# One bank pair and contiguous copies for the last remainder of a spectral stage, with a new order of the stages around it

## The chip, the cores and the metric

The kernel runs on one core of a Trainium2 chip. The metric is the device time of one execution in microseconds. Five engines work side by side, each through its own list of instructions in order: PE (matrix products; "PEld" is its weight load), DVE and ACT (element-wise work, and the copies out of PSUM), POOL (element-wise work in SBUF) and SP, which here only issues DMAs. PSUM has eight banks; the kernel uses them as four pairs, named 0, 2, 4 and 6 by their first bank.

## The reference

One block with two halves: a filter in the frequency domain, and a gated feed-forward network, each with a residual.

```python
def _A_ref(x, w_r, w_i):
    X = rfft2(x.astype(float32))
    X = X * (w_r + 1j * w_i)
    return irfft2(X, s=(S, D)).astype(bfloat16)

def _B_ref(x, w_gate, w_up, w_down):
    return (gelu(x @ w_gate) * (x @ w_up)) @ w_down

h  = x + _A_ref(layernorm(x), w_r, w_i)
h2 = h + _B_ref(layernorm(h), w_gate, w_up, w_down)
```

S is 2048 rows, D 576 columns, the hidden width 4608; everything is bf16.

## The kernel before

The two-dimensional transform and its inverse are done as matrix products with cosine and sine tables, in stages; the feed-forward half follows.

**First stage** (order SEQ1): the rows are normalized and multiplied by ATAB into U. It ends near 20 us.

**Forward stage** (order SEQF, 16 tiles i = 0 to 15, GORD[i] is the frequency group). A capital letter issues the first part of a step's products, the small letter the second part and the copy out of PSUM. D and d (10 products of 288 columns) turn U into CUS. B (4 products) turns CUS into YS. T (two DVE instructions, L673) multiplies YS by the filter weights WS: the first 256 columns go to TP, the last 32 of the 288 to TR, where four tiles i stand side by side. V and v (two times 8 products of 128 columns, L681) turn TP into the main part of the inverse's input, V. R and r (L697) do the same for the remainder, TR, four tiles at once. The lists DENG, BENG, VENG and RENG say which engine copies (`ev`, L606): a V copy is either one instruction of 512 columns or two of 256, one each on ACT and DVE.

**The remainder.** Group 0 (tile 15, LAST) needs other tables than the others, so the last remainder is done in two steps: R3 for tiles 12 to 14, and R4 for tile 15 alone, on bank pairs of their own. Remainders 0 to 2 are copied to RB in one piece (128x256) and spread to VR by eight small DMAs each, three issued by SP and five by POOL. R3 and R4 are copied straight to VR: each tile takes two instructions of 32 partitions x 128 elements, ACT for tiles 12 and 15, DVE for 13 and 14. VR holds, per group, `[o][e][n]` with n (16 long) innermost; the source runs over n with e (4 long) innermost.

**Bank pairs.** A step of the forward stage that opens (D, B, V, R) takes the free pair that was named longest ago in SEQF; the small letter gives it back. The inverse stage does the same over SEQ (`SLOT`), and starts from the list `last`, which says in which order the pairs become free.

**Inverse stage** (order SEQ, row blocks c = 0 to 7): I (4 products, main part only, L829) and i (6 products, of which the last two read the remainder VR) give PS, which E copies to GS (engine by its suffix: A for ACT, D for DVE, S for half each). N and o (4 products each, L846) give the rows back; a adds them to XO on DVE (L852). s sums the squares (A: ACT, L855; D: DVE, L912), q and c make the reciprocal deviation (ACT, DVE), n normalizes into HN (L880; P: POOL, D: DVE), u and U transpose by products (L898), e copies to HT. G0 and G1 are the first gate and up products (L938) on the first four row blocks.

**Loads.** LOADS ties DMAs on SP to steps: with "hold", SP waits until the last product issued so far is done. In the inverse stage these are the ten parts of the feed-forward weights of slot 0 (parts 2 to 7 with I0, i1, N0, i3, o1, N3; parts 8 and 9 with o3) and the tables DP and ITD (with i7). The first product of G0 needs all ten parts. Row blocks 8 to 15 of the inverse are done later, between the gate and up products.

After G1 the feed-forward half runs four blocks of 512 rows: gate and up products (L938), their gelu and multiply, and the down products (L1038).

Of the kernel before, what the change touches and what calls it, by code (L numbers as in the profile page):

```python
# [4 lines left out]
BF16 = mybir.dt.bfloat16  # L5
# [19 lines left out]
LORD = "x0-2 x2-4 a0-4 x4-8 a4-8 x8-12 x12-16 a8-16".split()  # L25
SPLIT = tuple(int(w[1:-1]) for w in SEQ1 if w[0] == "F")
ACT_TILES = tuple(int(w[1:]) for w in SEQ1 if w[0] == "Q")
SEQF = """D0 D2 d0 D1 d2 d1 D3 B0 d3 B2 D5 B1 d5 D6 T0 B3 d6 T1 D4 V0 T2 d4 D8 v0 B5 d8 T3 D7 T5 B4 d7 V2 V1 v2 v1 D9 B6 T4 d9 D11 B8 d11 D10 B7 T6 d10 V3 V4 v3 R0 v4 r0 V6 T7 B9 v6 D12 B10 d12 T8 T9 R1 D13 r1 d13 V5 B11 v5 T11 D15 B12 d15 V7 V8 v7 D14 T10 v8 d14 B13 T12 R2 V10 r2 v10 B15 T13 B14 T15 V11 V9 v11 V12 v9 v12 T14 V15 V13 v15 V14 v13 v14 R3 R4 r3 r4""".split()
VENG = [('act', 'dve'), ('dve',), ('act',), ('act', 'dve'), ('act', 'dve'), ('act', 'dve'), ('act', 'dve'), ('act',), ('act', 'dve'), ('act',), ('act', 'dve'), ('act',), ('act',), ('act', 'dve'), ('act', 'dve'), ('act', 'dve')]
DENG, BENG = ['act', 'dve', 'act', 'dve', 'act', 'act', 'act', 'act', 'act', 'act', 'act', 'dve', 'act', 'act', 'act', 'act'], ['act', 'act', 'act', 'act', 'act', 'dve', 'act', 'act', 'act', 'act', 'dve', 'act', 'act', 'act', 'act', 'act']  # L30
LOADS = {"r0": "t", "v12": "0", "v15": "1", ".I0": "2", ".i1": "3", ".N0": "4", ".i3": "5", ".o1": "6", ".N3": "7", ".o3": "8 9", ".i7": "d"}
RENG = ['act', 'act', 'dve', 'act', 'act']
QR = ((0, 1), (1, 2), (2, 3), (3, 4), (4, 8), (8, 16))
DEF0, DSTEP = 3, 4
SEQ = """I0 I1 I2 i0 i1 E0S i2 N0 E1D I3 o0 i3 E2A N1 a0 N2 E3S o1 s0A o2 I5 a1 N3 i5 o3 a2 a3 q0 s1A I7 I6 c0 i6 s2D E5A q1 E6A i7 I4 N5 i4 o5 E7A N6 c1 n0P u0 q2 s3D E4A n1P o6 q3 U0 a5 c2 u1 e0A N4 U1 e1A c3 n3P n2D o4 u2 U2 N7 a6 u3 o7 a4 a7 U3 e2A G0 e3D G1""".split()


def _np_bf16(a):
# [8 lines left out]
def build_tables():  # L47
# [7 lines left out]
    T = {}  # L55
# [44 lines left out]
    for st in range(2):  # L100
        g = 1 - st
        for p in range(128):
            half, r, jj = p // 64, (p % 64) // 4, p % 4
            low = (g + 16 * jj) if half == 0 else _minus_rows(g)[jj]
            k = 128 * r + low
            w = np.exp(-2j * np.pi * ((k * nn) % 2048) / 2048.0)
            if low in (0, 64):
# [3 lines left out]
                c = np.conj(w)  # L111
# [220 lines left out]
def _build(nc, A_x, A_w_r, A_w_i, B_w_gate, B_w_up, B_w_down, out):  # L332
    P = Prog(nc)
    T = build_tables()
    dram = {n: nc.inline_tensor(_np_bf16(T[n]), name="c_" + n.lower()) for n in T}
    PE, DVE, ACT, SP, POOL = "pe", "dve", "act", "sp", "pool"
# [3 lines left out]
    sb = SbufMap(nc, base, top)  # L340
# [12 lines left out]
    VR = sb.alloc("VR", [128, NG, 2, 4, NT], BF16)  # L353
# [57 lines left out]
    TR = sb.alloc("TR", [128, 2, 2, 2, 128], BF16)  # L411
# [66 lines left out]
    GORD = list(range(1, NG)) + [0]  # L478
# [102 lines left out]
    for w in SEQ1:  # L581
        a = w[1:]
# [6 lines left out]
    LAST = NG - 1  # L589

    FB, used, busy = {}, {0: -8, 2: -7, 4: -6, 6: -5}, set()
    for t, w in enumerate(SEQF):
        k, i = w[0], w[1:].rstrip("abc")
        if k in "DBVR":
            b = min((b for b in used if b not in busy), key=lambda b: used[b])
# [4 lines left out]
        elif k in "dvr":  # L600
            b = FB[k.upper(), int(i)]
# [3 lines left out]
    def ev(eng, dst, src, r, w):  # L605
        fn = (lambda v: v.tensor_copy(dst, src)) if eng == DVE else (lambda a: a.activation(dst, src, ACTF.Copy))  # L606
        P.op(eng, fn, r=r, w=w)
# [68 lines left out]
    def st_V(i, second, engs):  # L676
        g, z, b0 = GORD[i], i % NZ, FB["V", i]

        def mm(h, o, ct, first, last, after):
            c, t_ = ct  # L680
            return P.op(PE, lambda t: t.matmul(bank(b0 + o, 0, 128, 128 * c, 128 * c + 128), TP[64 * h:64 * h + 64, z, o, t_, c:256:2], VT[64 * h:64 * h + 64, 0 if g else 1 + o, t_, :],  # L681
                                               start=first, stop=last), r=[("T", z), "VT"], w=[("PS", b0 + o)], after=after)

# [6 lines left out]
            ev(e, v5[:, n * a:n * a + n], banks(b0 + a, n, 256).rearrange("p a (c e) -> p a c e", e=4), [("PS", b0 + a + k) for k in range(n)], [("V", g, a + k) for k in range(n)])  # L690

    def st_R(q, second):
        js = [i for i in range(4 * q, 4 * q + 4) if i < LAST] if q < 4 else [LAST]
        g0, n, b0 = GORD[js[0]], len(js), FB["R", q]

        def mm(h, o, t_, first, last, after):
            return P.op(PE, lambda t: t.matmul(bank(b0 + o, 0, 128, 0, 128), TR[64 * h:64 * h + 64, min(q, 3) % 2, o, t_, :], VT[64 * h:64 * h + 64, 3 if q < 3 else 1 + o if q == 4 else 0, t_, :], start=first, stop=last),  # L697
                        r=[("TR", min(q, 3) % 2, j) for j in range(4)] + ["VT"], w=[("PS", b0 + o)], after=after)

        halves(("R", q), second, [[0, 1]] * 2, mm)  # L700
# [99 lines left out]
    vkeys = vmain + vtail  # L800


    SLOT, last, held, ing = {}, [-4, -3, -2, -1], set(), False
    for t, w in enumerate(SEQ):
        k, i = w[0], int(w[1:].rstrip("ADSP"))
        if k in "INu":
            b = min((b for b in range(2 * ing, 4) if b not in held), key=lambda b: last[b])
# [3 lines left out]
        elif k in "ioUEae":  # L811
            b = SLOT[{"i": "I", "o": "N", "U": "u", "E": "I", "a": "N", "e": "u"}[k], i] // 2
# [4 lines left out]
        elif k == "G":  # L817
            ing = True
# [131 lines left out]
    def gu_first(i):  # L950
        for a in range(4):
# [104 lines left out]
    for tb in range(4):  # L1056
# [26 lines left out]
        for w in "0 1 0 2 1 3 2 3".split() if tb < 3 else "0 1 0 2 1 2".split():  # L1083
            first = ("Z", tb, int(w)) not in ends
# [39 lines left out]
```

## Time and profile before

| | us |
|---|---|
| median of 3 runs (488.22 to 489.38) | 489.23 |
| profiled execution, device time | 489.5 |
| its span | 487.7 |
| PE busy | 477.5 (98%) |
| DVE busy | 185.0 (38%) |
| ACT busy | 147.9 (30%) |
| POOL busy | 53.0 (11%) |

Busy shares are means over the whole span; the first 60 us, where the change lies, look quite different from the feed-forward half. A PE that is busy is not at its peak: products are pipelined, and their ends are modelled. In rows by stretch, each engine's busy time stands with its count of instructions, and after them the granted clock of PE as a share of full speed, the DMA share and the GB/s. In rows by group, after the bar, stand the total busy time, the mean of one in ns, and the idle time before them with what ended it.

### The profile page before, as it was taken

The page shows a single profiled execution, that of the slowest core. Times are in us where ns is not written, and L with a number is a line of the kernel's source. Part 1 is how long each engine was busy: PE and PEld are TensorE (multiplying, and loading weights), DVE is VectorE, ACT ScalarE, POOL GpSimd, SP SyncE. Part 2 cuts the span into 40 slices and gives each one's busy share as a digit, 9 for nine tenths or more (in the row PEclk, how much of TensorE's full clock was granted, in tenths as well). Part 3 has the DMA queues.
Part 4 walks back from the last instruction along what each step waited for, and adds up shares of the span by engine and source line. Part 5 has one row for each costly group of instructions (what it writes and reads, how often), then busy time and mean ns, then how long its engine had stood idle before and what let it go on. Part 6 is the DMA issues. An engine that isn't in the chain of part 4 may idle for free.

```text
span 487.7 us, 12880 instructions
## 1 busy us (share of the span) xinstructions
PE 477.5 (98%) x5871; PEld 279.1 (57%) x5872; DVE 185.0 (38%) x367; ACT 147.9 (30%) x294; POOL 53.0 (11%) x87
## 2 busy tenths in 40 slices
PE   7997999999999999999999999999999999999998
PEld 3876765554477744444577644444677444444774
DVE  7897845656511134333300144333101233333011
ACT  6997754343400023233200022332100123323000
POOL 6873226010120000000000000000000000000000
PEclk9998999999999999999999999999999999999999
DMA  8954688971250001100000001000000000000000
GB/s 291 215 138 147 202 280 247 389 158 26 98 175 25 15 24 23 23 0 1 1 15 13 27 21 23 13 1 2 1 15 26 14 1 0 1 1 1 3 26 26
DMA packets 26966, 33.06 MB, mean 68 GB/s; under 512 B 12560, under 2 KB 19104, under 8 KB 26912
## 3 DMA queue, kind: packets, MB, share of 16 engines
q1 hardware_dynamic: 23248, 19.74, 14.7%
q0 software_dynamic: 3664, 12.50, 7.9%
q8 instruction: 46, 0.75, 0.7%
q14 instruction: 8, 0.07, 0.0%
HBM read 26.08 MB, written 2.36 MB: 58 GB/s over the span
## 4 chain that ended last, share of the span: by engine, by line
PE 94%; DMA 1%; DVE 1%; POOL 1%; SPq 0%; issue 0%; POOLq 0%; DVEq 0%
PE PS L938 57%; PE PS L1038 27%; PE PS L640 2%; PE PS L1050 2%; PE PS L681 2%; DMA XO<-in_A_x_dram 1%; PE PS L551 1%; PE PS L660 1%; PE PS L829 1%; PE PS L988 1%; DVE XO L852 1%; DVE VR L606 1%; POOL HN L880 1%; SPq L242 0%; PE PS L1005 0%; PE PS L846 0%
## 5 line engine op out<-in xcount | busy, mean ns | idle before, releaser
L938 PE MATMUL PS<-HT,WG 64*128 64x512 bf16 (+1 forms) x2142 | 233.3, 372 | 0.0
L946 ACT ACTIVATE GL<-PS 128x512 bf16<-128x512 f32 x144 | 85.7, 596 | 281.6 <-PE PS L938 281.6
L938 PEld LDWEIGHTS PS<-HT,WG 64*128 64x128 bf16 x2142 | 105.0, 94 | 115.1 <-DVE AT L947 0.2
L947 DVE TENSOR_TENSOR AT<-GL,PS 128x512 bf16<-128x512 bf16 x144 | 98.9, 687 | 165.7 <-ACT GL L946 165.7
L1038 PE MATMUL PS<-WD,AT 64*128 64x288 bf16 x2160 | 132.9, 283 | 0.0
L1038 PEld LDWEIGHTS PS<-WD,AT 64*128 64x128 bf16 x2160 | 102.5, 94 | 30.6
L1025 DVE TENSOR_TENSOR OS<-PS,XO 128x288 bf16<-128x288 f32 (+2 forms) x32 | 13.2, 453 | 125.5 <-PE PS L1038 118.0
L938 PE MATMUL PS<-HT,WGX 64*128 64x512 bf16 x486 | 53.4, 376 | 0.0
L938 PEld LDWEIGHTS PS<-HT,WGX 64*128 64x128 bf16 x486 | 23.0, 94 | 29.4
L855 ACT ACTIVATE OS<-XO,NM 128x576 bf16<-128x576 bf16 x14 | 10.8, 774 | 11.4 <-DVE XO L1009 11.4
L640 PE MATMUL PS<-FT,U 64*128 64x288 bf16 x160 | 13.2, 283 | 0.0
L551 PE MATMUL PS<-ATS,XO 128*128 128x128 bf16 x96 | 8.2, 219 | 2.9 <-POOL ATS L520 1.9
L673 DVE TENSOR_TENSOR TP<-YS,WS 128x1024 bf16<-128x1024 bf16 x16 | 11.0, 687 | 0.0
L562 ACT ACTIVATE U<-PS 128x384 bf16<-128x384 f32 (+2 forms) x31 | 10.5, 421 | 1.2 <-PE PS L551 0.9
L494 DVE BATCH_NORM_STATS2 ST<-XO 128x6 f32<-128x288 bf16 x26 | 9.9, 442 | 1.9 <-DMA XO<-in_A_x_dram 1.9
L829 PE MATMUL PS<-DT,V 64*128 64x288 bf16 x64 | 7.2, 333 | 3.0 <-DVE VR L606 2.9
L681 PE MATMUL PS<-VT,TP 64*128 64x128 bf16 x256 | 9.7, 217 | 0.0
L242 POOL DMA_DIRECT2D WG<-in_B_w_gate_dram x9 | 6.1, 679 | 33.1 <-DMA WG<-in_B_w_gate_dram 29.6
L242 POOL DMA_DIRECT2D WD<-in_B_w_down_dram x9 | 6.7, 757 | 25.4 <-PE PS L1005 25.4
L551 PEld LDWEIGHTS PS<-ATS,XO 128*128 128x128 bf16 x96 | 6.9, 98 | 4.3 <-POOL ATS L520 2.8
L606 ACT ACTIVATE YS<-PS 128x576 bf16<-128x576 f32 x14 | 9.0, 657 | 0.3 <-PE PS L660 0.2
L1050 PE MATMUL PS<-WD,AT 128*128 128x448 bf16 (+1 forms) x72 | 9.0, 286 | 0.0
(89 smaller groups left out, 237.8 us busy)
## 6 DMA issues: line engine op xcount, KB each, us to landing
WD<-in_B_w_down_dram POOLq DMA_DIRECT2D x9, 576.0 KB, 11.4
WG<-in_B_w_up_dram SPq DMA_DIRECT2D x6, 576.0 KB, 6.9
WG<-in_B_w_gate_dram POOLq DMA_DIRECT2D x6, 576.0 KB, 5.8
out_dram<-OS SPq DMA_DIRECT2D x30, 72.0 KB, 1.7
XO<-in_A_x_dram SPq DMA_DIRECT2D x3, 576.0 KB, 7.3
WG<-in_B_w_gate_dram SPq DMA_DIRECT2D x4, 288.0 KB, 3.5
WG<-in_B_w_up_dram SPq DMA_DIRECT2D x4, 288.0 KB, 3.4
WGX<-in_B_w_up_dram SPq DMA_DIRECT2D x2, 576.0 KB, 4.7
```

The lines of the kernel that those rows point to most:

```text
L242: fn = lambda e: e.dma_start(out_ap, in_ap)
L551: P.op(PE, lambda t, b=b, lhs=lhs, p0=p0, p1=p1, s=s, e=e, o=o, c=c: t.matmul(bank(b, p0, p1, o, o + 128), lhs, ATS[:, c, :], start=s, sto ...
L606: fn = (lambda v: v.tensor_copy(dst, src)) if eng == DVE else (lambda a: a.activation(dst, src, ACTF.Copy))
L640: return P.op(PE, lambda t: t.matmul(bank(b0 + o, 0, 128, 0, 2 * HK), U[64 * h:64 * h + 64, us, 2 * i:2 * i + 2, :, :], FT[64 * h:64 * h + ...
L681: return P.op(PE, lambda t: t.matmul(bank(b0 + o, 0, 128, 128 * c, 128 * c + 128), TP[64 * h:64 * h + 64, z, o, t_, c:256:2], VT[64 * h:64 ...
L829: e[o] = P.op(PE, lambda t, r0=r0, o=o, j=j, lhs=lhs: t.matmul(bank(b + o, 0, 128, 0, KW), lhs, DT[r0:r0 + 64, 2 * o + j if j < 2 else 4, ...
L938: op = P.op(PE, lambda t, h0=h0, kt=kt, wt=wt, b=b, s=(not second and j == 0), e=(second and j == n - 1): t.matmul(bank(b, 0, 128, c0, c1) ...
L946: P.op(ACT, lambda a: a.activation(GL[:, s2, :], bank(b0), ACTF.Gelu_apprx_tanh), r=[("PS", b0)], w=[("GL", s2)])
L947: P.op(DVE, lambda v: v.tensor_tensor(AT[:, f, :], GL[:, s2, :], bank(b0 + 1), op=ALU.mult), r=[("GL", s2), ("PS", b0 + 1)], w=[("AT", f)])
L1025: P.op(DVE, lambda v: v.tensor_tensor(OS[:, p % 2, d0:d1], bank(b, 0, 128, 0, d1 - d0), XO[:, c, d0:d1], op=ALU.add), r=[("PS", b), ("X", ...
L1038: e[h] = P.op(PE, lambda t, f=f, h=h, r0=r0, j=j: t.matmul(bank(b0 + h, 0, 128, 0, 288), AT[r0:r0 + 64, f, 128 * p:128 * p + 128], WD[r0:r ...
L1050: P.op(PE, lambda t, b=b, d0=d0, d1=d1, f=f, j=j: t.matmul(bank(b, 0, 128, 0, d1 - d0), AT[:, f, 128 * p:128 * p + 128], WD[:, f, d0:d1], ...
```

## The change

1. R3 now holds all four tiles, 12 to 15, and R4 is gone. Its products run twice over TR: part 0 with the table of the other groups into columns 0 to 127 of the bank pair, part 1 with the tables of group 0 into columns 128 to 255; tile 15 is copied from part 1. The number of products is the same.
2. VTAB gets six blocks instead of four, since all remainder tables are now kept in the order `[e][n]`. With that, the copies to VR read 64 contiguous columns and write 64 contiguous elements.
3. `last`, the order in which the inverse stage takes the pairs, is computed from the forward stage.
4. SEQF, its engine lists and SEQ are new orders of the same steps. In SEQ, one more E is split over both engines, all four n go to POOL, one s moves from DVE to ACT, and i7 (with DP and ITD) now stands ahead of o3 (with parts 8 and 9).

```diff
-SEQF = """D0 D2 d0 D1 d2 d1 D3 B0 d3 B2 D5 B1 d5 D6 T0 B3 d6 T1 D4 V0 T2 d4 D8 v0 B5 d8 T3 D7 T5 B4 d7 V2 V1 v2 v1 D9 B6 T4 d9 D11 B8 d11 D10 B7 T6 d10 V3 V4 v3 R0 v4 r0 V6 T7 B9 v6 D12 B10 d12 T8 T9 R1 D13 r1 d13 V5 B11 v5 T11 D15 B12 d15 V7 V8 v7 D14 T10 v8 d14 B13 T12 R2 V10 r2 v10 B15 T13 B14 T15 V11 V9 v11 V12 v9 v12 T14 V15 V13 v15 V14 v13 v14 R3 R4 r3 r4""".split()
+SEQF = """D2 D0 d2 D1 d0 d1 B2 D5 B0 d5 T2 D3 B1 d3 D4 T0 T1 B5 d4 D8 B3 d8 D7 T3 B4 d7 V0 D6 v0 V1 T5 d6 v1 R0 V2 r0 v2 T4 B6 D9 B8 T6 V3 d9 D11 v3 d11 B7 D10 B9 d10 V6 V4 T7 v6 v4 V5 B10 v5 R1 D12 T8 r1 d12 B11 T9 V7 D14 v7 T10 d14 D13 B12 d13 D15 T11 V9 T12 d15 v9 V8 B13 v8 R2 r2 T13 B14 T14 B15 V12 V10 v12 v10 V13 V11 T15 v13 V14 v11 v14 V15 R3 v15 r3""".split()
...
-RENG = ['act', 'act', 'dve', 'act', 'act']
+RENG = ['dve', 'act', 'act', 'act', 'act']
...
-SEQ = """I0 I1 I2 i0 i1 E0S i2 N0 E1D I3 o0 i3 E2A N1 a0 N2 E3S o1 s0A o2 I5 a1 N3 i5 o3 a2 a3 q0 s1A I7 I6 c0 i6 s2D E5A q1 E6A i7 I4 N5 i4 o5 E7A N6 c1 n0P u0 q2 s3D E4A n1P o6 q3 U0 a5 c2 u1 e0A N4 U1 e1A c3 n3P n2D o4 u2 U2 N7 a6 u3 o7 a4 a7 U3 e2A G0 e3D G1""".split()
+SEQ = """I0 I1 I2 i0 E0S i1 E1S i2 E2A N0 I3 o0 i3 N1 I4 o1 a0 E3S N2 o2 a1 s0A q0 i4 a2 s1A I7 c0 N3 E4S q1 s2D i7 I6 o3 E7A i6 c1 N4 o4 a3 q2 E6A c2 N7 I5 o7 a4 n0P N6 s3A a7 i5 n1P n2P q3 c3 o6 u1 U1 u2 E5A u0 U2 a6 n3P e1A e2D U0 N5 u3 e0A o5 a5 U3 G0 e3D G1""".split()
...
     def st_R(q, second):
-        js = [i for i in range(4 * q, 4 * q + 4) if i < LAST] if q < 4 else [LAST]
-        g0, n, b0 = GORD[js[0]], len(js), FB["R", q]
...
-            return P.op(PE, lambda t: t.matmul(bank(b0 + o, 0, 128, 0, 128), TR[64 * h:64 * h + 64, min(q, 3) % 2, o, t_, :], VT[64 * h:64 * h + 64, 3 if q < 3 else 1 + o if q == 4 else 0, t_, :], start=first, stop=last),
...
+        js = range(4 * q, 4 * q + 4)
+        b0 = FB["R", q]
...
+            part, t_ = pt
+            return P.op(PE, lambda t: t.matmul(bank(b0 + o, 0, 128, 128 * part, 128 * part + 128), TR[64 * h:64 * h + 64, q % 2, o, t_, :], VT[64 * h:64 * h + 64, 4 + o if part else 3, t_, :], start=first, stop=last),
...
-                dst = VR[64 * t_ + 32 * (j % 2):64 * t_ + 32 * (j % 2) + 32, g, :, :, :].rearrange("p o e n -> p o n e")
-                src = PS[32 * j:32 * j + 32, b0 * 512:(b0 + 2) * 512].rearrange("p (a c) -> p a c", a=2)[:, :, 64 * t_:64 * t_ + 64].rearrange("p a (n e) -> p a n e", e=4)
+                dst = VR[64 * t_ + 32 * (j % 2):64 * t_ + 32 * (j % 2) + 32, g, :, :, :].rearrange("p o e n -> p o (e n)")
+                src = PS[32 * j:32 * j + 32, b0 * 512:(b0 + 2) * 512].rearrange("p (a c) -> p a c", a=2)[:, :, 128 * (i == LAST) + 64 * t_:128 * (i == LAST) + 64 * t_ + 64]
                 ev((ACT, DVE, DVE, ACT)[j], dst, src, keys, [("V", g, 2 + t_)])
...
-    SLOT, last, held, ing = {}, [-4, -3, -2, -1], set(), False
+    SLOT, last, held, ing = {}, [sorted(used.values()).index(used[2 * b]) - 4 for b in range(4)], set(), False
```

DENG, BENG and VENG also change: of the 32 copies of D and B, DVE makes four instead of five; of the V copies, it makes three whole ones instead of one, and ACT four instead of five.

More of the change, by code (lines that the diff above doesn't have):

```diff
@@ L27 @@
 ACT_TILES = tuple(int(w[1:]) for w in SEQ1 if w[0] == "Q")
-SEQF = """D0 D2 d0 D1 d2 d1 D3 B0 d3 B2 D5 B1 d5 D6 T0 B3 d6 T1 D4 V0 T2 d4 D8 v0 B5 d8 T3 D7 T5 B4 d7 V2 V1 v2 v1 D9 B6 T4 d9 D11 B8 d11 D10 B7 T6 d10 V3 V4 v3 R0 v4 r0 V6 T7 B9 v6 D12 B10 d12 T8 T9 R1 D13 r1 d13 V5 B11 v5 T11 D15 B12 d15 V7 V8 v7 D14 T10 v8 d14 B13 T12 R2 V10 r2 v10 B15 T13 B14 T15 V11 V9 v11 V12 v9 v12 T14 V15 V13 v15 V14 v13 v14 R3 R4 r3 r4""".split()
-VENG = [('act', 'dve'), ('dve',), ('act',), ('act', 'dve'), ('act', 'dve'), ('act', 'dve'), ('act', 'dve'), ('act',), ('act', 'dve'), ('act',), ('act', 'dve'), ('act',), ('act',), ('act', 'dve'), ('act', 'dve'), ('act', 'dve')]
@@ L30 @@
-DENG, BENG = ['act', 'dve', 'act', 'dve', 'act', 'act', 'act', 'act', 'act', 'act', 'act', 'dve', 'act', 'act', 'act', 'act'], ['act', 'act', 'act', 'act', 'act', 'dve', 'act', 'act', 'act', 'act', 'dve', 'act', 'act', 'act', 'act', 'act']
+SEQF = """D2 D0 d2 D1 d0 d1 B2 D5 B0 d5 T2 D3 B1 d3 D4 T0 T1 B5 d4 D8 B3 d8 D7 T3 B4 d7 V0 D6 v0 V1 T5 d6 v1 R0 V2 r0 v2 T4 B6 D9 B8 T6 V3 d9 D11 v3 d11 B7 D10 B9 d10 V6 V4 T7 v6 v4 V5 B10 v5 R1 D12 T8 r1 d12 B11 T9 V7 D14 v7 T10 d14 D13 B12 d13 D15 T11 V9 T12 d15 v9 V8 B13 v8 R2 r2 T13 B14 T14 B15 V12 V10 v12 v10 V13 V11 T15 v13 V14 v11 v14 V15 R3 v15 r3""".split()
@@ L31 @@
+VENG = [('act',), ('act', 'dve'), ('act', 'dve'), ('act', 'dve'), ('act', 'dve'), ('dve',), ('act', 'dve'), ('act', 'dve'), ('dve',), ('act', 'dve'), ('act',), ('dve',), ('act',), ('act', 'dve'), ('act',), ('act', 'dve')]
+DENG, BENG = ['act', 'dve', 'act', 'act', 'act', 'act', 'act', 'act', 'dve', 'act', 'act', 'act', 'act', 'act', 'act', 'act'], ['act', 'dve', 'act', 'act', 'act', 'act', 'act', 'dve', 'act', 'act', 'act', 'act', 'act', 'act', 'act', 'act']
 LOADS = {"r0": "t", "v12": "0", "v15": "1", ".I0": "2", ".i1": "3", ".N0": "4", ".i3": "5", ".o1": "6", ".N3": "7", ".o3": "8 9", ".i7": "d"}
-RENG = ['act', 'act', 'dve', 'act', 'act']
+RENG = ['dve', 'act', 'act', 'act', 'act']
@@ L154, in build_tables @@
     assert np.allclose(VN[0, 0], VN[0, 1])
-    T["VTAB"] = np.stack([VN[0, 0], VN[1, 0], VN[1, 1], VN[0, 0].reshape(128, 4, 16, 4).transpose(0, 1, 3, 2).reshape(128, 256)], 1).reshape(128, -1)
+    T["VTAB"] = np.stack([VN[0, 0], VN[1, 0], VN[1, 1]] + [v.reshape(128, 4, 16, 4).transpose(0, 1, 3, 2).reshape(128, 256) for v in (VN[0, 0], VN[1, 0], VN[1, 1])], 1).reshape(128, -1)
     kr = np.arange(1, K2)
@@ L389, in _build @@
     BT = sb.alloc("BT", [128, 2, 2, 128], BF16)
-    VT = sb.alloc("VT", [128, 4, 2, 128], BF16)
+    VT = sb.alloc("VT", [128, 6, 2, 128], BF16)
     end1 = sb.off
@@ L692, in st_R, with mm @@
     def st_R(q, second):
-        js = [i for i in range(4 * q, 4 * q + 4) if i < LAST] if q < 4 else [LAST]
-        g0, n, b0 = GORD[js[0]], len(js), FB["R", q]
[L696 to L700, printed above, removed]
+        js = range(4 * q, 4 * q + 4)
+        b0 = FB["R", q]
+        def mm(h, o, pt, first, last, after):
+            part, t_ = pt
+            return P.op(PE, lambda t: t.matmul(bank(b0 + o, 0, 128, 128 * part, 128 * part + 128), TR[64 * h:64 * h + 64, q % 2, o, t_, :], VT[64 * h:64 * h + 64, 4 + o if part else 3, t_, :], start=first, stop=last),
+                        r=[("TR", q % 2, j) for j in range(4)] + ["VT"], w=[("PS", b0 + o)], after=after)
+        halves(("R", q), second, [[(part, t_) for part in range(1 + (q == 3)) for t_ in range(2)]] * 2, mm)
         if not second:
```

## The prediction

> **What bounds the kernel now.** I read the busy times by stretch first, to find the stage that the change touches and what is idle in it.
>
> ```profile
> core 0: us, PE busy (x) PEld busy (x) DVE busy (x) ACT busy (x) POOL busy (x), PEclk, DMA share, GB/s
> 20.10:43.50 23.40, 23.40 (x522) 18.37 (x520) 22.24 (x54) 22.45 (x50) 17.00 (x32) 1.00 0.63 159
> 43.50:46.45 2.95, 0.07 (x4) 0.00 (x1) 2.78 (x5) 2.78 (x4) 0.00 (x0) 0.91 0.55 195
> 46.45:59.03 12.58, 12.04 (x184) 8.58 (x186) 9.22 (x19) 8.36 (x19) 3.58 (x3) 0.89 0.69 204
> 134.30:487.70 353.40, 351.02 (x4178) 199.95 (x4172) 91.61 (x150) 65.09 (x109) 3.15 (x4) 1.00 0.06 18
> ```
>
> The rows are the forward stage, the hand-over, the inverse stage up to the first gate/up product, and most of the rest. Outside the hand-over PE never rests for long, so a microsecond taken out before 59.03 reaches the end as a microsecond, unless a transfer catches up. Next the chain of waits (start, length, what):
>
> ```profile
> 42.79 0.74 DVE V L606 x2
> 43.55 0.68 DVE VR L606
> ...
> 45.64 0.70 DVE VR L606
> 46.34 0.14 issue
> 46.48 3.38 PE PS L829 x30
> ```
>
> PE stands still while DVE makes four copies of the last remainder, one after the other (the middle two are left out). The timeline gives the neighbours:
>
> ```profile
> 42.83 0.74 PE L697 MATMUL PS<-VT,TR 64*128 64x128 bf16 x16
> 43.50 2.83 ACT L606 ACTIVATE VR<-PS 32x128 bf16<-32x128 f32 x4
> 46.48 2.10 PE L829 MATMUL PS<-DT,V 64*128 64x288 bf16 x16 [2.91 <-DVE VR L606]
> ```
>
> The remainder's products end at 43.57; I0, the first inverse product, starts at 46.48. I0 reads only the main part V, complete at 42.79 + 0.74 = 43.53. It waits because its banks are the ones that these copies read. Counting bank pairs through the old order, R3 sits on pair 0 and R4 on pair 2, the last two to come free, and I0 and I1 take 0 and 2. The idle time also costs clock:
>
> ```profile
> 45.50:46.00 0.50, 0.00 (x0) 0.00 (x0) 0.49 (x2) 0.49 (x2) 0.00 (x0) 0.89 0.00 0
> 48.50:49.00 0.50, 0.50 (x8) 0.37 (x5) 0.17 (x1) 0.13 (x1) 0.00 (x0) 0.50 0.73 230
> 49.00:49.50 0.50, 0.50 (x10) 0.37 (x7) 0.29 (x1) 0.28 (x1) 0.00 (x0) 0.70 0.54 207
> ```
>
> The granted clock falls to half near 45.9 (0.89 is 22% of that row at half) and is back near 49.3 (0.70 is 60% at half). Over the inverse stage it averages 0.89: 0.11 x 12.58 = 1.38 us lost.
>
> **The change part by part.** *The bank line itself* changes nothing here: by the new order the pairs are last named in the order 0, 2, 4, 6, so the formula gives the old list -4, -3, -2, -1. What counts is that the new order puts R3, now all four remainders, on pair 6. I0, I1, I2 take pairs 0, 2, 4, and pair 4 holds V15, which I0 needs anyway.
>
> *Start of I0.* The new tail is V14 v11 v14 V15 R3 v15 r3. R3 and r3 hold 16 products, as R3, R4, r3, r4 did, so I keep 43.57 as their end. v15 ends before r3's eight products:
>
> ```profile
> 26.18 0.22 PE PS L681 x8
> L606 ACT ACTIVATE V<-PS 128x256 bf16<-128x256 f32 x10 | 3.8, 398 | 0.1
> L606 DVE CAST V<-PS 128x256 bf16<-128x256 f32 x10 | 4.0, 422 | 0.6 <-PE PS L681 0.2
> ```
>
> Its two half copies start near 43.57 - 0.22 = 43.35 and end near 43.8; with the 0.14 of issue above, I0 starts at 43.95: **-2.53**. Bounds: -2.7 if they end with r3, -1.9 if ACT, nearly full in the forward row, is one 512-wide copy (0.62) behind.
>
> *Clock.* The new gap is about 0.4 us, and the clock lasted 2.3 us of the old one (43.57 to 45.9): **-1.38**, between that and 0. [...]
>
> *Forward order.* Products, copies and multiplies of the stage are the same in number; ACT keeps 28 of the 32 576-wide copies instead of 27 and DVE 4 instead of 5, while DVE takes three whole V copies instead of one. By the rows above the two carry 22.45 and 22.24 of 23.40 us, so nothing is there to win but what PE loses to waits. At the chain's 0.61 us per ten products of D, 0.24 per four of B, 0.22 per eight of V and 0.11 per four of R:
>
> ```profile
> 24.45 0.24 PE PS L660 x4
> 24.69 0.61 PE PS L640 x10
> 34.16 0.11 PE PS L697 x4
> ```
>
> 16 x (0.61 + 0.24 + 0.44) + 10 x 0.11 = 21.7 us of work stand in 23.4. I take **0**, from -1.0 (more than half the waits) to +1.5 (as many again). The larger table VTAB (six blocks of 64 KB instead of four) queues on SP ahead of pieces of WS:
>
> ```profile
> 36.20 0.33 SPq L242 DMA_DIRECT2D DT<-c_dtab  x1
> 38.26 0.68 DVE L673 TENSOR_TENSOR TP<-YS,WS 128x1024 bf16<-128x1024 bf16 x1
> ```
>
> SP issues DT once the last doubled piece of WS has landed, 36.2; T12, the first multiply to need it, runs at 38.26. 128 KB more, 0.8 us at the forward row's 159 GB/s, is covered by these two microseconds; without them it would cost its 0.8.
>
> *Copies of the remainder.* I0 to I2 are 12 products, then two pairs of i0 follow, at 0.25 us for four:
>
> ```profile
> 50.10 0.25 PE PS L829 x4
> L606 ACT ACTIVATE VR<-PS 32x128 bf16<-32x128 f32 x4 | 2.8, 696 | 0.1
> L606 DVE CAST VR<-PS 32x128 bf16<-32x128 f32 x4 | 2.7, 686 | 0.1
> L606 DVE CAST RB<-PS 128x256 bf16<-128x256 f32 x1 | 0.4, 425 | 0.0
> L606 ACT ACTIVATE V<-PS 128x512 bf16<-128x512 f32 x5 | 2.8, 621 | 0.0
> ```
>
> So i0 wants the remainder at 43.95 + 1.0 = 44.95. The copies have 128 elements per partition in single-element steps; the RB copy has twice as many, in runs of 64, and takes 0.425. From ACT's 398 and 621 for 256 and 512 elements, 128 in a run come to 398 - 111 = 0.29 us. Four per engine from 43.8: 44.95 at 0.29, 45.5 at 0.425, 46.6 at 0.69. I take 0.29, an estimate from these rows. [...]
>
> Remainder 2 travels by DMA and comes second here:
>
> ```profile
> 39.82 2.44 POOL L242 DMA_DIRECT2D VR<-RB  x5 [1.25 <-DVE RB L606]
> DMA to landing us min/median/max: 1.9/2.9/3.7
> ```
>
> Between r2 and the end of its stage stand 12 half V, two B and two double R in place of 13, two and four single R: 0.22 us less. The fifth issue moves from 41.8 (2.44/5 before the end) to 42.0 and lands 2.9 later, 44.9, or at 3.7 at 45.7. Either way some 0.14 of issue later i0 goes on, at 45.1: **+0.2**, from 0 to +0.9.
>
> *Inverse order.* All four normalizations of the first block go to POOL; before, one was DVE's.
>
> ```profile
> 54.02 1.35 POOL L880 TENSOR_SCALAR HN<-XO,NM,RS 128x640 bf16<-128x640 bf16 x1 [11.76 <-DVE RS L865]
> L880 POOL TENSOR_SCALAR HN<-XO,NM,RS 128x640 bf16<-128x640 bf16 x3 | 3.6, 1192 | 12.1 <-DVE RS L865 11.9 <-POOL HN L880 0.2
> ```
>
> The first stood 54.02 - 46.48 - 1.38 = 6.16 us after I0. The new order has one add (0.75) less ahead of c0 on DVE and the 0.2 above: 5.7. Four at 1.19 with 0.18 between them take 5.3; then u3, o5 and U3 (0.13 + 0.45): first gate product 11.6 us after I0 at full clock. Before, it was 12.55 - 1.38 = 11.17, plus the 0.2 just counted: **+0.25**, from -0.3 (a bound by products alone) to +0.7. That is 43.95 + 11.6 = 55.55.
>
> *Weights for that product.* Ten loads of slot 0 hang on products of this stage through SP. The order moves DP and ITD (after i7) ahead of the last two (after o3).
>
> ```profile
> 53.07 0.53 SPq L242 DMA_DIRECT2D WG<-in_B_w_gate_dram  x1
> 53.64 0.60 SPq L242 DMA_DIRECT2D WG<-in_B_w_up_dram  x1
> 54.64 0.33 SPq L242 DMA_DIRECT2D DP<-c_dpar  x1
> 55.01 0.43 SPq L242 DMA_DIRECT2D ITD<-c_idef  x1
> WG<-in_B_w_up_dram SPq DMA_DIRECT2D x1, 144.0 KB, 4.8
> ```
>
> Before, the last landed at 53.64 + 4.8 = 58.44, 0.6 ahead of its reader at 59.03. Now 88 products to i7 put the hold at 43.95 + 5.4 + 0.5 = 49.85; DP, ITD and the ninth part go at 49.95, 50.3 and 50.75, the last at 51.3. At 4.8 it lands at 56.1, with 4.4 (the ninth's row) at 55.7. I take 56.0 and 0.1 of issue: **+0.55**, from 0 to +1.9 (472 KB in front at 350 GB/s add 1.35).
>
> **Sum:** -2.53 - 1.38 + 0 + 0.2 + 0.25 + 0.55 = -2.9 us. The first gate product moves from 59.03 to about 56.1. The profiled execution took 489.5 us (span 487.7), the median of the runs is 489.23; the median less 2.9 is 486.3.
>
> **The rivals.** *Copies no shorter* (0.69 comes from 32 partitions at a time, not from the steps; no row parts the two): they end at 46.6, i0 goes on at 46.7 instead of 45.1. The four normalizations follow, the weights' wait vanishes in it: +1.6 - 0.55, time 487.4. Against it: RB's run form.
> [...]
> *Forward stage longer:* full ACT and DVE queues turn the order into waits, +1.5, 487.8.
> *Slower, by the weights:* the last part of slot 0 decides as soon as it lands after 59.0, 7.7 us after its issue. This profile has a load that took so long when the queue was full:
>
> ```profile
> VT<-c_vtab SPq DMA_DIRECT2D x1, 256.0 KB, 8.0
> ```
>
> At 8.0 it lands at 59.3; PE starts 0.4 later than before: 489.6. Against it: DMA share 0.69 in the stage, and 4.8 as the worst part.
>
> **How the numbers follow.** Main case 0.58 (485.3 to 487.3); copies no shorter 0.12; half clock 0.10; forward stage 0.12; slower 0.08. The range 485.0 to 488.2 holds the first four nearly whole; what it leaves out is the slower case and the outer ends. About 0.3%, 1.5 us, is what a measurement here can tell from no change; the line is 487.76. Main and the copies give faster 0.70 less a little, half clock and forward stage lie at the line and give half: faster 0.79, within 0.13, slower 0.08.
>
> **What would show it.** I0 some 0.4 us after the last remainder product, at a granted clock of 1.00 from 43 to 56; VR copies of 32x128 near 0.29 us; i0's remainder product released by a DMA or a VR copy near 45; u3 released by POOL; the first gate product released by the last load of WG, near 56. Wrong would be: a PE gap over 1 us at the hand-over, VR copies at 0.69, a forward stage off by more than 1 us, or time given back after 59.

## The result and the profile after

| | before | after |
|---|---|---|
| median of 20 runs, us | 489.81 | 487.69 |
| ratio, 95% interval | | 0.9967 (0.9951 to 0.9982) |
| profiled execution, us | 489.5 | 487.7 |
| its span | 487.7 | 485.9 |
| first product of G0 in it | 59.03 | 57.22 |

The ratio is a gain of 1.6 us: the direction and the range hold, but it is little more than half of the 2.9 us forecast. In a later set of seven executions of the new kernel one took 1298.32 us, at a granted clock of 1.000 and with no trace kept; no ratio counts it, and why it happened stays open. Here is the chain of waits of the new kernel (start, length, what) from the last remainder to the first gate product. L830 is the old L829, L939 the old L938.

```profile
43.45 0.22 PE PS L698 x8
43.67 0.28 PE PS L681 x8
43.96 0.42 DVE V L606
44.38 0.14 issue
44.52 1.16 PE PS L830 x16
45.68 0.06 issue
45.74 1.08 PE PS L830 x14
...
51.78 0.39 SPq L242
52.17 0.04 issue
52.22 4.96 DMA WG<-in_B_w_up_dram
57.17 0.05 issue
57.22 2.79 PE PS L939 x47
```

I0 no longer waits for a copy of the remainder; the one copy in the chain is half of tile 15's main part. i0 follows after 0.06 us. From 51.78 on, a transfer sets the end instead of an engine. PE's own timeline gives the gaps and where U3, the last transpose, ends (55.84 + 0.22 = 56.06):

```profile
43.75 0.39 PE L698 MATMUL PS<-VT,TR 64*128 64x128 bf16 x8
44.52 1.16 PE L830 MATMUL PS<-DT,V 64*128 64x288 bf16 x16 [0.38 <-DVE V L606]
...
55.84 0.22 PE L899 MATMUL PS<-IDT,HN 64*128 64x64 bf16 x4
57.22 4.97 PE L939 MATMUL PS<-HT,WG 64*128 64x256 bf16 x80 [1.16 <-DMA WG<-in_B_w_up_dram]
```

So the hand-over gap went from 2.91 to 0.38, and 1.16 us of waiting stands before G0. The groups by form show the copies and the normalizations, and POOL's timeline when the latter ran:

```profile
L881 POOL TENSOR_SCALAR HN<-XO,NM,RS 128x640 bf16<-128x640 bf16 x4 | 3.5, 870 | 8.2 <-DVE RS L866 8.1 <-POOL HN L881 0.2
...
L606 DVE CAST VR<-PS 32x128 bf16<-32x128 f32 x4 | 1.1, 286 | 0.1
L606 ACT ACTIVATE VR<-PS 32x128 bf16<-32x128 f32 x4 | 1.1, 264 | 0.0
```

```profile
50.42 0.86 POOL L881 TENSOR_SCALAR HN<-XO,NM,RS 128x640 bf16<-128x640 bf16 x1 [6.95 <-DVE RS L866]
52.09 0.87 POOL L881 TENSOR_SCALAR HN<-XO,NM,RS 128x640 bf16<-128x640 bf16 x1 [0.80 <-DVE RS L866]
...
54.32 0.87 POOL L881 TENSOR_SCALAR HN<-XO,NM,RS 128x640 bf16<-128x640 bf16 x1 [0.32 <-DVE RS L866]
```

The busy times by stretch, in the columns known from before:

```profile
20.10:43.50 23.40, 23.03 (x509) 17.92 (x506) 21.59 (x53) 22.08 (x48) 17.53 (x32) 1.00 0.69 167
43.50:44.50 1.00, 0.64 (x24) 0.46 (x17) 0.84 (x3) 0.88 (x3) 0.00 (x0) 1.00 0.14 25
...
56.00:57.00 1.00, 0.06 (x5) 0.00 (x0) 0.96 (x2) 0.98 (x2) 0.00 (x0) 1.00 0.11 33
```

The granted clock is 1.00 throughout, and in 56 to 57 PE is idle. The first row still has 509 products where the old one had 522: the forward stage is behind. SP's timeline shows the queue that the last weights stood in:

```profile
50.33 0.33 SPq L242 DMA_DIRECT2D WG<-in_B_w_up_dram  x1
50.70 0.43 SPq L242 DMA_DIRECT2D DP<-c_dpar  x1
51.17 0.43 SPq L242 DMA_DIRECT2D ITD<-c_idef  x1
51.65 0.52 SPq L242 DMA_DIRECT2D WG<-in_B_w_gate_dram  x1
52.22 0.60 SPq L242 DMA_DIRECT2D WG<-in_B_w_up_dram  x1
```

The first line is part 7, the last two are parts 8 and 9. DP and ITD stand ahead of these; part 9 leaves at 52.22 and lands 4.96 later.

### The profile page after: what moved, and what is told of

Read it like the earlier page. It is cut to its first block, busy times and chain, and to the rows that moved or that the text cites. A ratio compares the mean times of both kernels' runs of the same rounds, so it can differ in the third digit from the quotient of the medians.

```text
span 485.9 us, 12883 instructions
## 1 busy us (share of the span) xinstructions
PE 476.7 (98%) x5872; PEld 279.4 (57%) x5872; DVE 182.9 (38%) x366; ACT 146.6 (30%) x295; POOL 52.8 (11%) x88
## 4 chain that ended last, share of the span: by engine, by line
PE 93%; DMA 1%; DVE 0%; issue 0%; SPq 0%; DVEq 0%
PE PS L939 58%; PE PS L1039 27%; PE PS L1051 2%; PE PS L640 2%; PE PS L681 2%; DMA WG<-in_B_w_up_dram 1%; PE PS L830 1%; PE PS L660 1%; PE PS L989 1%; PE PS L847 1%; PE PS L1006 0%; PE PS L698 0%; DVE CUS L606 0%; DVE V L606 0%; SPq L242 0%
## 5 line engine op out<-in xcount | busy, mean ns | idle before, releaser
L939 PE MATMUL PS<-HT,WG 64*128 64x512 bf16 (+1 forms) x2142 | 233.3, 372 | 1.2 <-DMA WG<-in_B_w_up_dram 1.2
L939 PEld LDWEIGHTS PS<-HT,WG 64*128 64x128 bf16 x2142 | 105.2, 94 | 116.1 <-DMA WG<-in_B_w_up_dram 1.3
L939 PE MATMUL PS<-HT,WGX 64*128 64x512 bf16 x486 | 53.4, 376 | 0.0
L939 PEld LDWEIGHTS PS<-HT,WGX 64*128 64x128 bf16 x486 | 23.2, 94 | 29.2
L856 ACT ACTIVATE OS<-XO,NM 128x576 bf16<-128x576 bf16 x15 | 11.6, 774 | 11.4 <-DVE XO L1010 11.4
L640 PE MATMUL PS<-FT,U 64*128 64x288 bf16 x160 | 13.5, 284 | 0.3 <-DVE CUS L606 0.3
L606 ACT ACTIVATE CUS<-PS 128x576 bf16<-128x576 f32 x14 | 9.0, 653 | 0.8 <-PE PS L640 0.7
```

What stands on the lines that cost most here:

```text
L640: return P.op(PE, lambda t: t.matmul(bank(b0 + o, 0, 128, 0, 2 * HK), U[64 * h:64 * h + 64, us, 2 * i:2 * i + 2, :, :], FT[64 * h:64 * h + ...
L856: P.op(ACT, lambda a, c=c, out=out: a.activation(out, XO[:, c, 0:D], ACTF.Square, bias=NM[:, c:c + 1], accum_out=SB2[:, 1, c:c + 1]), r=[( ...
L939: op = P.op(PE, lambda t, h0=h0, kt=kt, wt=wt, b=b, s=(not second and j == 0), e=(second and j == n - 1): t.matmul(bank(b, 0, 128, c0, c1) ...
```

## The experiments

All differences of a few tenths are read from traces, in four pieces: the forward stage (first product of D to the end of the last remainder product), the gap to I0, I0 to the end of U3, and the wait of the first gate product. From the start of that product to the end of PE's last one it is 426.30 us in every trace, within 0.01, except in e7 (427.95), where the clock falls in it. A negative wait is a modelled end that reaches past the next start. The edits behind the names follow below.

| trace | forward | gap | I0 to U3 | wait | sum |
|---|---|---|---|---|---|
| before, profiled first | 23.46 | 2.91 | 12.72 | -0.17 | 38.92 |
| before again (a_before) | 23.46 | 2.92 | 11.42 | 0.28 | 38.07 |
| before again (a2_before) | 23.46 | 2.91 | 12.64 | -0.16 | 38.85 |
| after | 23.84 | 0.38 | 11.54 | 1.16 | 36.92 |
| after again (a_after) | 23.25 | 0.38 | 11.53 | 1.37 | 36.53 |
| e1 tables last | 23.26 | 0.38 | 11.55 | 0.06 | 35.25 |
| e2 parts early | 23.66 | 0.38 | 11.67 | 0.06 | 35.76 |
| e3 table split | 24.19 | 0.33 | 11.53 | 1.28 | 37.33 |
| e4 both | 25.24 | 0.38 | 11.68 | 0.06 | 37.36 |
| e5 table twice | 24.13 | 0.38 | 11.65 | 1.31 | 37.48 |
| e6 contiguous copies alone | 24.05 | 1.31 | 11.42 | -0.16 | 36.62 |
| e7 all but contiguous copies | 24.81 | 0.38 | 13.14 | 1.49 | 39.81 |
| e8 I0 waits for the remainder | 23.96 | 1.58 | 11.26 | 1.17 | 37.97 |
| e9 both of these | 25.08 | 3.19 | 12.87 | 0.49 | 41.64 |
| f1 before, table of six | 23.46 | 2.91 | 11.42 | -0.16 | 37.63 |
| f2 after, table of four | 23.25 | 0.38 | 11.54 | 1.00 | 36.17 |
| f3 f2 and parts early | 23.24 | 0.38 | 11.80 | 0.06 | 35.49 |
| f4 e6, table of four | 23.94 | 1.31 | 11.41 | 0.14 | 36.81 |

Ratios are to the kernel before, with their 95% intervals.

**Both kernels again.**

> The kernel before, once more, for a second trace of it. Theory 'larger table': the first doubled piece of WS is issued some 1.1 us after the first D product, as in the first trace (20.52 and 19.38 after the first load), against 1.3 to 2.5 in the traces of the changed kernels. Rival 'spread of executions': the landing of WS moves by a microsecond from one execution of the same kernel to the next, and this trace falls among the changed ones. The gap at the hand-over is 2.9 again; the clock falls in it or, as in 3 to 4 of the 15 runs beside the first experiments (granted clock 1.00 as a mean), it does not.

> The changed kernel, once more, timed on this chip. Gap at the hand-over 0.38, wait for part 9 at the first gate product near 1.2, no fall of the clock between; the time from the first gate product to the end 426.31 as in all traces so far. Against before some 1.6 to 2.1 us less.

> The kernel before, for a third trace. The third doubled piece of WS was issued at 27.72 and 27.46 in the first two, the forward stage lasted 23.46 in both. If the pieces of WS move with the execution and not with the kernel, this trace may lie anywhere up to 30.4 and 25.2; if the changed kernels bring their own delay, it is near 27.6 and 23.5 again. The gap at the hand-over is 2.9; the clock falls in it in three of four executions.

They took 488.91 (one execution), a median of 488.64 (ratio 0.9958, 0.9938 to 0.9979) and 491.61 (one execution). The first of them differs from the trace shown before in one thing that matters. Its busy times by stretch:

```profile
43.50:46.50 3.00, 0.30 (x8) 0.12 (x6) 2.95 (x5) 2.92 (x5) 0.00 (x0) 1.00 0.59 197
...
46.45:58.40 11.95, 10.90 (x184) 7.88 (x184) 9.55 (x21) 8.90 (x20) 3.58 (x3) 1.00 0.77 215
```

The chain of waits of the same run:

```profile
46.58 0.14 issue
46.71 2.01 PE PS L829 x30
...
52.71 5.65 DMA WG<-in_B_w_up_dram
58.36 0.05 issue
58.40 1.70 PE PS L938 x27
```

The same kernel, with the same gap of 2.9 us, kept its full clock here. Its inverse stage then takes 11.42, not 12.72, and it is already the weights, on their way for 5.65, that release G0.

**The weights' wait.** e1 puts the tables behind the weights, e2 hangs the two parts on an earlier step:

```diff
-LOADS = {... ".N3": "7", ".o3": "8 9", ".i7": "d"}
+LOADS = {... ".N3": "7", ".o3": "8 9 d"}       # e1
+LOADS = {... ".N3": "7 8 9", ".i7": "d"}       # e2
```

> The changed kernel with the tables DP and ITD moved behind parts 8 and 9 of the weights (both after o3). In the changed kernel PE stands still for 1.16 us at 57.22 until part 9, issued at 52.22, lands at 57.17. Theory 'tables in front': the two tables cost 0.43 of issue time on SP and some 0.5 of transfer, so part 9 is issued near 51.8, lands near 56.3, and the first gate product starts near 56.4: 0.8 us less than the changed kernel. Rival 'full queue': the transfers of parts 6 and 7 fill the queue and only the issue time is won: 0.4 us less. Rival 'hook': o3 itself is too late, nothing is won.

> The changed kernel with parts 8 and 9 tied to N3, with part 7, and the tables left at i7 behind them. Theory 'last load of the weights decides': parts 8 and 9 go out near 50.7 and 51.2, land before 56.1, and the first gate product follows U3 at about 56.1 without a wait: 1.1 us less than the changed kernel. Rival 'full queue': the bytes ahead of part 9 are the same (the share of DMA is 0.92 from 50 to 54), it lands no earlier than 57, and at most 0.2 is won.

Medians 487.32 (0.9944, 0.9924 to 0.9965) and 487.12 (0.9942, 0.9920 to 0.9964). The chain of e2 at the same place:

```profile
56.47 0.06 PE PS L899 x4
56.52 0.06 issue
56.58 3.43 PE PS L939 x59
```

U3 releases G0 in both, 0.06 us after its end. So the wait came from the place in SP's queue: with parts 8 and 9 ahead of the 472 KB of tables, or hung on an earlier step, it is gone. The traces give 1.1 to 1.3 us for it, and so do the ratios against that of after (0.0023 and 0.0025, 1.1 to 1.2 us). Against the second measurement of after (0.9958) they give 0.7 to 0.8, and all these intervals overlap: the size rests on the traces.

**The table in the forward stage.** e3 loads blocks 4 and 5 of VTAB only after the pieces of WS, e4 joins it with e2, e5 loads all of VTAB a second time ahead of them, f1 loads six blocks in the old kernel (two unused), f2 gets by with four in the new one (tile 15's main part uses the permuted tables, and its copy undoes the permutation).

```diff
-    P.dma(SP, VT[:, :, :, :]..., dram["VTAB"][:, :], "vt", w=["VT"])
+    P.dma(SP, VT[:, 0:4, :, :]..., dram["VTAB"][:, 0:1024], "vt", w=["VT"])
...
+    P.dma(SP, VT[:, 4:6, :, :]..., dram["VTAB"][:, 1024:1536], "vt2", w=["VT2"])
```

> The changed kernel with the two new blocks of VTAB loaded behind the pieces of WS instead of ahead of them (they are first read by the last remainder). In the changed kernel all pieces of WS land 1.0 to 1.3 us later than before, DVE's copy of WS starts at 22.04 instead of 20.99, T waits 0.47 us for a doubled piece, and the last remainder product ends near 44.1 instead of 43.57. Theory 'larger table': DVE's copy is back near 21.0, the wait of T goes, the forward stage ends near 43.6, and everything behind, the weights' loads too, moves by 0.5 us: 0.5 less than the changed kernel. Rival 'new order': the stage still ends near 44.1, nothing is won.

> Both edits, parts 8 and 9 tied to N3 and the two blocks of VTAB loaded late. If the two losses are separate, they add: first gate product near 55.5, 1.6 us less than the changed kernel, some 3.4 less than before, which is what was forecast (2.9) plus the weights' wait counted in it (0.55). Rival: the weights land late again once PE is earlier, and no more than 1.2 is won.

> The changed kernel with VTAB (384 KB) loaded a second time, right behind the first, into space that is free then: three times the change's 128 KB more in front of the pieces of WS. Theory 'larger table': the pieces land 2 to 3 us later than in the changed kernel, the third doubled piece is issued after 30.5 (28.96 and 27.32 in its two traces), and the forward stage lasts 25 us or more. Rival 'spread of executions': the issue stays between 27.3 and 30.4, the bounds of all traces so far, and the stage between 23.2 and 25.2.

> The kernel before with VTAB of six blocks, all loaded where the four were, the two new ones unused; orders, banks and copies as before. In the three traces of before the forward stage lasted 23.46 us each time; in ten traces of kernels with the new forward order 23.25 to 25.24, mean 24.14, and in the one with the old order but the larger table 24.05. Theory 'larger table': forward stage 23.7 or more in this trace, 0.4 to 0.7 more than before in the mean. Rival 'new forward order': 23.5 and no more than 0.2.

> The changed kernel with VTAB of four blocks again: the main part of group 0 uses the tables in the order of the remainder, and its two half copies (V15) read PSUM in the other order. Theory 'larger table': the forward stage is back at 23.2 to 23.5, 0.4 to 0.7 less than the changed kernel; the wait for part 9 stays. Rival 'new forward order': 24 or more, nothing is won. If V15's copies take longer by their read (0.4 before), I0 starts that much later.

Medians and ratios: e3 488.14 (0.9958, 0.9937 to 0.9978), e4 487.37 (0.9950, 0.9928 to 0.9972), e5 489.63 (0.9998, 0.9974 to 1.0021), f1 490.03 (0.9998, 0.9985 to 1.0010), f2 487.53 (0.9947, 0.9929 to 0.9964). The splits shorten nothing, where 0.5 us (e3) and 1.6 us (e4) less than after were expected, and bring a wait of their own; e4 has the longest forward stage of them all, and its waits (engine, tile, line, releaser: sum, times, longest) say why:

```profile
DVE WS L729 <- DMA WS<-in_A_w_r_dram: 1.4, 1, 1.4
...
DVE TP L674 <- DMA WS<-WS: 1.1, 1, 1.1
...
PEld PS L699 <- DMA VT<-c_vtab: 1.0, 1, 1.0
```

The filter weights WS come late, and so do the multiplies that read them; the late half of the table then holds up a remainder for 1.0 us. In the trace of after, the same two waits are shorter:

```profile
DVE WS L728 <- DMA WS<-in_A_w_r_dram: 0.9, 1, 0.9
...
DVE TP L673 <- DMA WS<-WS: 0.5, 1, 0.5
```

With four blocks (f2, f3) neither is there and the stage takes 23.25, but a_after has six and takes 23.25 too, and f1 shows the old order untouched by them. e5's 384 KB cost 1.5 us against after by the ratios, whose intervals just overlap, with a forward stage inside the spread of the others. So long forward stages go with late pieces of WS: where the last doubled piece lands within 16.1 us of the first product of D (the three traces of before, a_after, e1, f2, f3), the stage takes 23.24 to 23.46, and where it lands 16.8 us after it or later, 23.66 to 25.24, but for f1 (17.2, and 23.46). f4, with 16.6 and 23.94, stands between. Whether the 128 KB of the change make the pieces late stays open: f2's interval overlaps that of after, f1 has six blocks and no longer stage, and e6 and f4, with the old order, run long. f4 was expected at 486.6 and came out 0.5 above it.

**Which part brings the gain.** e6 is the old kernel, old orders and R4 included, with the contiguous copies alone (the two table blocks that they need come behind the pieces of WS, as in e3); f4 is e6 with a table of four. e7 is the new kernel with the old copies. e8 makes the first inverse product wait for the whole remainder, as the shared bank pairs made it; e9 is e7 and e8.

```diff
-  dst = VR[...].rearrange("p o e n -> p o n e")
-  src = PS[...]...[:, :, 64 * t_:64 * t_ + 64].rearrange("p a (n e) -> p a n e", e=4)
+  dst = VR[...].rearrange("p o e n -> p o (e n)")
+  src = PS[...]...[:, :, 64 * t_:64 * t_ + 64]
```

```diff
-  r=vk[j] + ["DT"], ...
+  r=(vkeys if c == 0 else vk[j]) + ["DT"], ...    # e8
```

> The kernel before with nothing but the contiguous copies to VR (R3 and R4, bank pairs and both orders as before; the two new table blocks are loaded behind the pieces of WS). The copies end 1.6 us earlier, so the gap at the hand-over is 1.3 instead of 2.9 and the clock falls seldom or never. Theory 'weights next': parts 8 and 9 are tied to o3, which comes early in this order, so PE reaches the first gate product 1.6 (no fall before) to 3 us (a fall before) earlier, waits there for part 9 some 0.3 us or more, and the mean is 1.5 to 2.5 less than before: about as good as the whole change. Rival 'the order carries it': 0.5 or less.

> The kernel before with the contiguous copies alone, and with VTAB of four blocks (V15 as above; here it isn't the last to be copied). Gap at the hand-over 1.3, no wait for the weights. Theory 'larger table': forward stage 23.5, and 0.5 less than the same with six blocks (487.16 mean), about 486.6. If both orders are worth nothing by themselves, it is level with the changed kernel with early parts and four blocks, or within 0.3 of it.

> The changed kernel with the old form of the copies to VR (single-element steps; the last remainder's products use the tables in the old order for it). Theory 'steps': the copies take 0.69 instead of 0.27 to 0.29, the last ends 1.65 us later, and since the loads of the weights hang on PE's progress, all of it passes on: first gate product 1.4 to 1.7 later than in the changed kernel. Rival 'hidden by the weights': the wait of 1.16 takes most of it, 0.5 later. Rival '32 partitions': the copies stay near 0.28 and nothing changes.

> The changed kernel with I0 waiting for the whole remainder, as it did through its banks, with the short copies. Gap at the hand-over 1.6 instead of 0.38; I0 to U3 0.25 shorter, since i0 finds the remainder ready; so PE reaches the first gate product 0.9 later, the loads shift with it: 0.6 to 0.9 more than the changed kernel. With the strided copies the same wait cost 1.8 more from the first D to the first gate product (41.64 against 39.81), 1.5 of it a fall of the clock. Rival: the weights hide it, 0.2 or less.

> The changed kernel with the old form of the copies, and with I0 waiting for the whole remainder as it did through its banks. This puts the old hand-over into the new order: gap near 3.1 us instead of 0.38, and I0 to U3 some 0.3 shorter, so 2.4 more at full clock; if the clock falls in the gap as in the trace of before, 3.8 more. If the forward order had a share of the gain, it would stay below before by that share.

Medians and ratios: e6 487.15 (0.9933, 0.9902 to 0.9965), f4 487.15 (0.9942, 0.9922 to 0.9962), e7 490.55 (0.9998, 0.9981 to 1.0015), e8 488.52 (0.9979, 0.9961 to 0.9996), e9 491.79 (1.0026, 1.0009 to 1.0042). In e6's chain the four copies still stand ahead of I0, short ones now, and the weights come in time:

```profile
44.12 0.28 DVE VR L607
...
45.01 0.30 DVE VR L607
45.31 0.14 issue
45.45 2.01 PE PS L830 x30
...
56.81 0.06 PE PS L899 x4
56.87 3.16 PE PS L939 x57
```

The copies alone bring as much as the whole change: the intervals of e6, f4 and after overlap. Without them (e7) I0 is early, but PE stops at i0 for the same copies:

```profile
45.55 1.16 PE L830 MATMUL PS<-DT,V 64*128 64x288 bf16 x16 [0.38 <-DVE V L606]
48.38 0.34 PE L830 MATMUL PS<-DT,VR 64*128 64x288 bf16 x2 [1.67 <-DVE VR L606]
```

So the stage from I0 to U3 is 1.60 us longer than that of after, and a wait of 1.49 before G0 stays. (The profile puts it down to a copy to HT on DVE that ends at 60.17; but in the other traces of the new order G0 starts before this copy has ended, and here part 9 lands at 60.13, G0 starting at 60.18.) Given short copies, early banks are worth the 1.20 us between the gaps of e8 and after, less 0.28 that e8 wins back from I0 to U3, where i0 finds the remainder ready: 0.9 us. The ratios show 0.0012 (0.6 us), inside the intervals. e9, which has the new orders and neither of the two gains, is 1.3 us slower than the old kernel by its ratio.

**The best version.** f3 is f2 with parts 8 and 9 hung on N3, as in e2.

> The same with parts 8 and 9 tied to N3. If table and weights are the two losses, this is 1.5 to 1.8 less than the changed kernel: about 486.3, 0.7% under before.

Median 486.32, ratio 0.9924 (0.9907 to 0.9940): 3.7 us under the kernel before. Its interval lies below that of the first comparison of after; it touches that of the second (from 0.9938), and it overlaps those of e1, e2, e6, f2 and f4. That 486.3 is also the time forecast for the change itself is chance: the runs of before beside it stand at 490.37, not 489.23.

## Why the prediction was right or wrong, step by step

**Start of I0: right.** Forecast 0.4 us after the last remainder product, measured 0.38: -2.53, to the hundredth. The absolute time, 44.52 instead of 43.95, is 0.19 of a later first stage and 0.38 of a longer forward stage.

**Copies of the remainder: right.** Forecast 0.29, measured 0.264 and 0.286, down from 0.696 and 0.686. e7 shows that the steps are the cause: the same 32 partitions and 128 elements take 0.696 and 0.689 in it again. Both forms read 64 columns of PSUM in a row; what differs is the write to VR, in steps of 16 elements before. The two half copies of V15 in f2 and f3 read PSUM in single-element steps and write as ever, and the group with them keeps its mean (0.392 and 0.416 in f2 against 0.388 and 0.418); DVE's half alone takes 0.43 in f3's chain and 0.42 in that of after. So here the steps of the write cost (0.69 against 0.29), and those of the read hardly (0.43 against 0.42). i0's remainder product follows I0 after 1.22 us, forecast 1.15; a_before needs 0.98 from the one to the other. The 0.24 between them is the +0.2 of the forecast, and DVE's four copies, which end at 45.59, cause it. The rival of copies no shorter falls; e7 is what it would have been, and it would have cost the whole gain, not 1.05 us of it.

**Inverse order: the sum right by luck, against a wrong base.** Forecast 11.6 us from I0 to U3's end, measured 11.54, but not by the path of the forecast. The first normalization starts 5.90 after I0, not 5.7 (and the working, 6.16 - 0.75 + 0.2, adds to 5.61). The four take 0.87 each, not 1.19, with waits of up to 0.80 for the deviations between them, and last 4.77, not 5.3. From their end at 55.19 to the end of U3 it is 0.87, not 0.58. Nor does POOL hold up u3: the longest wait of PE that the trace shows between I0 and U3 is 0.20, for an add on DVE (L853). PE's own work fills this stage: it is busy for 11.08 of the 11.54. And the old stage at full clock takes 11.42 by the second trace of before, not 12.55 - 1.38 = 11.17: order and remainder cost 0.12 together, not 0.45. In e8, without the wait for the remainder, the new stage takes 11.26.

**Clock: the step that failed.** I took -1.38 from one trace, as if each execution of before lost it and none of after. A stretch of 3.4 us at half clock shows in a run's mean granted clock as 0.997 (the profiled run of before) or 0.996 (that of e1). Of 74 runs of before made beside the experiments, 12 have a mean clock of 1.000 and take 488.70 on average; the 49 with one such stretch take 490.25, and the 13 with a lower mean (0.993 or 0.990: two stretches or more, at 0.003 to 0.004 each) 491.34. Of 26 runs of after, 20 have none, and 6 have one still; of the first 20, those without take 487.54, the five with one 489.59. The falls of changed kernels need no hand-over: in the trace of e1 one comes at 13 us, in the first stage (0.82 from 13.0 to 13.5, 0.50 from 16.0 to 16.5), in that of e7 one begins at 60.2, as the wait for the weights ends (1.00 from 59.5 to 60.0, 0.66 from 60.0 to 60.5). At full clock on both sides the change is 487.54 - 488.70 = -1.2, against 2.9 - 1.38 = 1.5 forecast for it. The rest of the ratio, 1.6 - 1.2 = 0.4 us, is what rarer falls gave in that comparison; by the second one (0.9958, 2.1 us) it is 0.9. Counted directly, the falls cost before 490.19 - 488.70 = 1.5 us in the mean of its 74 runs and after 488.08 - 487.64 = 0.4 in that of its 26, a difference of 1.0. So the term was -0.4 to -1.0, and it was smallest in the comparison that the forecast was made for. Nor do the runs show half clock in every execution, to which 0.10 was given: 20 of the 26 runs of after have a mean clock of 1.000.

**Weights: right place, too small.** Forecast +0.55, measured a wait of 1.16 and in the second trace 1.37. Part 9 left at 52.22, not 51.3: 0.57 of that is the later I0; the rest arose on SP, which was at part 7 until 50.66 and so sent DP at 50.70. It took 4.96, not 4.7. And before is not free of the wait: at full clock G0 waited 0.28 there (-0.16 in f1). The landing, 57.17, stayed inside the bound of +1.9 (whose 350 GB/s is what the trace of before moves from 53 to 55: 348 and 353), and the slower rival, with its 8.0 us, did not come. In e1 and e2, with parts 8 and 9 ahead of the tables, the wait is gone.

**Forward order: 0 was too kind.** The seven traces with after's forward order and table (after, a_after, e1, e2, e7, e8, e9) run from 23.25 to 25.08 with a mean of 23.98, the four of before's order with its own copies stand at 23.46 each: +0.5, inside the bounds, and a third of what the rival of a longer forward stage asked for. I had called the larger table covered by the two microseconds ahead of T12. In the trace of after the wait came at other readers of the same queue: 0.89 at DVE's copy of WS, 0.47 at T5. It isn't shown that the order costs this: e6 and f4, with the old one, take 24.05 and 23.94.

At full clock, then: -2.53 for the gap; from I0 to the first gate product 12.70 and 12.90 after (11.54 + 1.16, 11.53 + 1.37) instead of 11.70 (a_before) and 11.26 (f1), which is +1.3 between the means; forward +0.09 by the two traces of after. The sum is -1.1, beside the -1.2 of the runs.

## What to carry to other kernels

Where a stage change stalls on copies, look at the step of the copy before the order of the work: a change of layout in a constant table brought as much as the whole change here (0.9933 and 0.9942 against 0.9967 and 0.9958). A term that comes from the clock must be weighed with the share of executions in which it falls, from several runs of both kernels (here 62 of 74 before and 6 of 26 after). And whoever makes a stage shorter has to look at its loads again: here the wait for the last one grew from 0.28 at the most to 1.16 and 1.37, and another order in the queue took 1.1 to 1.3 us of it out of the traces.

## What was not expected of the hardware

**The clock.** A PE gap of 2.91 us at the hand-over was followed by a stretch at half clock in two traces of before (45.9 to 49.3 in the profiled one; a2_before takes 12.64 from I0 to U3 where a_before takes 11.42) and by none in a_before and in f1, the old kernel with a larger table, with the same gap to 0.01 us. Nor does the stretch have to begin in the gap: e9, at a mean clock of 0.997, takes 12.87 from I0 to U3 against 11.26 in e8, 1.61 more, and the stretch in e7 cost 1.65 (427.95 against 426.30), so nearly all of that in e9 lies behind the gap. In e7 a wait of 1.49 stands ahead of the fall, while none follows the gap of 1.58 in e8. So the length of a gap alone does not decide here; what does is not shown.

**Issue order on SP.** 144 KB took 4.96 us to land behind DP and ITD and 5.65 in a_before, while the group of 288 KB loads in the same stage of after took 3.9 each by the median:

```profile
WG<-in_B_w_up_dram SPq DMA_DIRECT2D x3, 288.0 KB, 3.9
WG<-in_B_w_gate_dram SPq DMA_DIRECT2D x2, 288.0 KB, 3.9
...
DP<-c_dpar SPq DMA_DIRECT2D x1, 216.0 KB, 4.9
WG<-in_B_w_gate_dram SPq DMA_DIRECT2D x1, 144.0 KB, 4.3
WG<-in_B_w_up_dram SPq DMA_DIRECT2D x1, 144.0 KB, 5.0
```

So size alone does not set the time. In a_before no table stood ahead, so the tables alone do not set it either; what does was not tried apart.

**POOL.** The normalization of 128x640 took 0.87 us each in the new order and 1.19 on average in the old one (one of them 1.35), with the same shapes; why was not tried apart.
